# One PSUM pool, a fixed order in SyncE's queue, weights loaded early and masks by product in an RWKV-7 recurrence followed by a GELU layer

## The chip, the cores and the metric

One core of a Trainium2 chip runs the whole program. The metric is the time of one execution in microseconds (us), the median of the runs; beside it stands the span of a profiled execution, from its first instruction to its last.

## What is computed

The first half is a recurrence over 768 steps for 4 batches x 8 heads with a 40 x 40 state each, the second half a two-layer network on 3072 rows.

```python
for t in range(S):                                   # attention, per batch and head
    y[:, :, t] = np.einsum('bhd,bhde->bhe', rt, state)
    Sa = np.einsum('bhde,bhe->bhd', state, at)
    state_decay = state * wt[:, :, None, :] - np.einsum('bhd,bhe->bhde', Sa, bt)
    state = state_decay + np.einsum('bhd,bhe->bhde', vt, kt)
x = attn_out.transpose(0, 2, 1, 3).reshape(B * S, H * D)      # 3072 x 320
h = x @ w_in                                                  # 320 x 2048
out = (0.5 * h * (1.0 + erf(h / sqrt(2)))) @ w_out            # 2048 x 320
```

The two weight matrices arrive as 64-bit floats; the kernel loads their words and builds 32-bit floats on VectorE (`to_float`, seven instructions for each piece).

## The kernel before, in words

**Chunks.** The 768 steps are cut into 12 chunks of 64 (`NCH`). Inside a chunk the recurrence is written as products of small matrices: strictly upper triangular 64 x 64 blocks N, A, RV and M for each batch and head, made on TensorE in PSUM and masked on their way to SBUF (`masked`, line 313; the mask is `upper`), and the inverse of a unit triangular matrix made from N. Batches lie in pairs on the partitions (index e), heads in pairs (index x), so that one group of 32 products (64 hardware matmuls in the profile) handles all 32 batches and heads.

**Names.** `sums(c)` (L254) makes the running sum `cum` of log w and two exponentials of it. `turns(c)` (L286) transposes six tensors on TensorE (wT, aT, vT, nT, kT, rT), each copied from PSUM by ScalarE or VectorE, and starts the loads of v and r. `make_N`, `make_RV`, `make_A`, `make_av` are products that need the chunk's own data alone; `make_X`, `make_sa`, `make_M`, `make_y2`, `make_QY` and `outputs` need the state that the chunk before left. `turn_state` transposes the new state (tn). `up` is the first layer with GELU (ph, gt), `down(c, g)` the second for half of the rows (po, os).

**The inverse.** `make_N` sends N to DRAM (L345, 8 transfers) so that `invert` can read it back with one 32 x 32 block per partition (Nb, L377). GpSimd then does 62 instructions (L383, L385) on W, which goes to DRAM (inv, L389) and comes back as Tt and T2 (`fetch_inverse`, 12 transfers, L401 and L404). `corner` transposes a part of Tt on VectorE (L, L415) and multiplies (J); `joined` does the last products (J2) and completes Tt.

**What sets the order.** TensorE's instructions stand in the order of the program. All other engines, SyncE's queue of transfers among them, are ordered by the scheduler, which moves an instruction up when it can; each queue then runs in that order, and an instruction that waits holds all behind it. The loop over chunks (L591) is a software pipeline: in iteration c the state part of chunk c, the inverse of chunk n = c + 1, and the loads, sums and transposes of chunk c + 2.

**Memory.** PSUM holds three double banks for everything (`ps_duo`) and one for the two layers (`ps_fc`); `up` uses the halves of the latter's banks in turn (L552). `pad_ring` gives three padded tiles in turn to a, v, r and cs.

**Weights.** `first_weights` (L227) loads the five parts of w_in through a scratch of two and converts each; `second_weights` (L241) does the same for 16 parts of w_out through two buffers.

Of the kernel before, what the change touches and what calls it, by code (L numbers as in the profile page):

```python
# [11 lines left out]
INT32 = mybir.dt.int32  # L12
# [10 lines left out]
def kernel(  # L23
# [46 lines left out]
    P = 128  # L70
# [16 lines left out]
    ps_duo = ctx.enter_context(tc.tile_pool(name="ps_duo", bufs=3, space=PSUM))  # L87
    ps_fc = ctx.enter_context(tc.tile_pool(name="ps_fc", bufs=1, space=PSUM))

    def duo(name):  # L90
        return ps_duo.tile([P, 2, 512], FP32, tag="duo", name=name)
# [31 lines left out]
    pad_ring = ring("pad", 3, [P, G, H, HP], pads, nc.gpsimd)  # L123
# [14 lines left out]
    def fetch_padded(c, n, src, eng, placed):  # L138

        t = pad_ring()  # L140
# [10 lines left out]
    def load(c, other):  # L151
        fetch(c, "w", w, nc.sync)
        fetch_padded(c, "a", a, other, False)
        fetch(c, "k", k, nc.sync)
        fetch(c, "b", b, nc.sync)

    load(0, nc.scalar)
# [15 lines left out]
    mask = upper.bitcast(INT32)  # L173
# [5 lines left out]
    N_ring = ring("N", 1, [P, 2, G, NP, C], whole, nc.gpsimd)  # L179
    A_ring = ring("A", 1, [P, 2, G, NP, C], whole, nc.gpsimd)  # L180
    VR_ring = ring("VR", 2, [P, 2, G, NP, VC], lambda t: t.rearrange("p y g m c -> p (y g m) c")[:, :, D:], nc.gpsimd)
    SM_ring = ring("SM", 1, [P, 2, G, NP, VC], lambda t: t.rearrange("p y g m c -> p (y g m) c")[:, :, D:], nc.gpsimd)
# [26 lines left out]

    def to_float(dst, words):  # L210
# [16 lines left out]
    def first_weights():  # L227
        wide = moe_w_in.dtype != FP32
        src = (moe_w_in.bitcast(UINT32) if wide else moe_w_in).rearrange("k (p x j) -> k x p j", x=2, p=NF // 2)
        scratch = gt_tile().rearrange("p f t -> p (f t)").bitcast(UINT32)  # L230
        for kt in range(NK):
            dst = w_in_sb[:, kt]
            n = 2 * LW if wide else LW
            to = scratch[:, kt % 2 * n:(kt % 2 + 1) * n] if wide else dst
            for x, at, rows, feature in halves_of(kt):
                nc.sync.dma_start(out=to[x * HP + at:x * HP + at + rows].rearrange("p (f j) -> p f j", f=NF // 2),
                                  in_=src[feature:feature + rows, x])
            if wide:
                to_float(dst, to)

    def second_weights():  # L241
        wide = moe_w_out.dtype != FP32
        src = moe_w_out.bitcast(UINT32) if wide else moe_w_out
        for f in range(NF):
# [9 lines left out]
    def sums(c):  # L254
# [3 lines left out]
        for g in range(G):  # L258
            mm(cum[:, g], cum_m, logw[:, g].rearrange("p h d -> p (h d)"))
        rw = part_ring()[:, :, :DM]  # L260
        nc.scalar.activation(rw, cum, ACT.Exp, scale=-1.0)  # L261
        cs = pad_ring()
        nc.vector.tensor_copy(cs[:, :, :, :D], cum.rearrange("p g (h d) -> p g h d", h=H))  # L263
# [22 lines left out]
    def turns(c):  # L286
# [9 lines left out]
        fetch_padded(c, "v", v, nc.sync, True)  # L296
        v_ = raws.pop((c, "v"))
        VR = VR_ring()
        for g in range(G):
            nc.gpsimd.tensor_copy(VR[:, :, g, :, :D], v_[:, g, :, :D].rearrange("p (m y) d -> p y m d", y=2))  # L300
        vT = side("vT", "late", 1)
        nc.vector.tensor_copy(vT, flip(by_place(v_), "vT_ps"))
        nT = side("nT", "nT", 1)
        nc.scalar.copy(nT, flip(by_pair(nb), "nT_ps"))
        kT = side("kT", "kT", 1)
        nc.scalar.copy(kT, flip(by_pair(ks), "kT_ps"))
        fetch_padded(c, "r", r, nc.sync, True)
        rT = side("rT", "rT", 2)
        nc.vector.tensor_copy(rT, flip(by_place(raws.pop((c, "r"))), "rT_ps"))  # L309
        turned_in[c] = dict(ks=ks, nb=nb, wp=wp, aT=aT, vT=vT, nT=nT, kT=kT, rT=rT, VR=VR)  # L310


    def masked(to, pt):
        nc.vector.copy_predicated(to, mask.unsqueeze(1).to_broadcast([P, 2 * G * NP, C]), pt)
# [38 lines left out]
    def make_A(c):  # L353
        t = turned_in[c]
        A = t["A"] = A_ring()
# [13 lines left out]
    def invert(c):  # L369
# [9 lines left out]
        for j in range(BL - 1):  # L379
# [5 lines left out]
            nc.gpsimd.tensor_tensor(W[:, :rows, j + 1:], W[:, :rows, j + 1:], t, ALU.add)  # L385
        inv = dram.tile([2, 2, 2, G * NP, BL, BL], FP32, tag="inv", name="inv")
# [269 lines left out]
```

## Time and profile before

| what | value |
|---|---|
| median of 3 runs | 1113.56 us (1107.23 to 1120.38) |
| the profiled execution's own time | 1114.27 us |
| its span | 1112.3 us |
| TensorE busy | 796.9 us |
| VectorE, ScalarE, GpSimd busy | 311.6, 222.2, 339.4 us |
| mean granted TensorE clock | 0.86 |

A row of a timeline reads: start, duration, engine, line, operation, output<-inputs, partitions and shape, count, and in brackets the idle time before it with what ended it. Rows of the same kind that follow each other are merged. `SPq` is SyncE's queue: the time in which it issues transfers, not in which they run. A hardware matmul count is twice the program's, since a product of 32-bit floats runs as two. A row of waits reads: who waited, for whom, us in total, times, longest.

### The profile page before, as it was taken

The page shows a single profiled execution, that of the slowest core. Times are in us where ns is not written, and L with a number is a line of the kernel's source. Part 1 is how long each engine was busy: PE and PEld are TensorE (multiplying, and loading weights), DVE is VectorE, ACT ScalarE, POOL GpSimd, SP SyncE. Part 2 cuts the span into 40 slices and gives each one's busy share as a digit, 9 for nine tenths or more (in the row PEclk, how much of TensorE's full clock was granted, in tenths as well). Part 3 has the DMA queues.
Part 4 walks back from the last instruction along what each step waited for, and adds up shares of the span by engine and source line. Part 5 has one row for each costly group of instructions (what it writes and reads, how often), then busy time and mean ns, then how long its engine had stood idle before and what let it go on. Part 6 is the DMA issues. An engine that isn't in the chain of part 4 may idle for free.

```text
span 1112.3 us, 29772 instructions
## 1 busy us (share of the span) xinstructions
PE 796.9 (72%) x13256; PEld 637.2 (57%) x13256; DVE 311.6 (28%) x414; ACT 222.2 (20%) x282; POOL 339.4 (31%) x846
## 2 busy tenths in 40 slices
PE   4100565678878878788797787796886897787887
PEld 4100553476666665576585575675675685575765
DVE  2607495540140240240240240240330240240200
ACT  2000211211311311311311311311311311211110
POOL 5560036008007017016026026035035026025000
PEclk9555679779989989889889889889889889889899
DMA  5419452430330431331331331421321321111000
GB/s 90 86 35 130 96 132 69 97 71 13 68 69 13 72 72 21 61 73 19 63 68 22 65 63 24 70 56 27 68 54 25 68 57 22 25 44 21 16 19 13
DMA packets 255248, 60.41 MB, mean 54 GB/s; under 512 B 241232, under 2 KB 250960, under 8 KB 255120
## 3 DMA queue, kind: packets, MB, share of 16 engines
q1 hardware_dynamic: 251040, 56.22, 27.2%
q10 hardware_dynamic: 4080, 2.30, 1.0%
q8 instruction: 104, 1.70, 0.6%
q14 instruction: 24, 0.20, 0.1%
HBM read 44.30 MB, written 10.22 MB: 49 GB/s over the span
## 4 chain that ended last, share of the span: by engine, by line
PE 38%; POOL 20%; DMA 12%; SPq 11%; issue 9%; DVE 5%; ACT 4%; DVEq 0%; POOLq 0%; ACTq 0%
PE po L568 14%; POOL W L385 10%; POOL tmp L383 10%; PE ph L559 7%; SPq L146 3%; DMA Nb<-N 3%; SPq L345 2%; PE cum L100 2%; DMA pad<-in_r_dram 2%; SPq L401 2%; PE J L100 2%; DMA inv<-W 2%; PE N_ps L100 2%; ACT gt L556 2%; DMA Tt<-inv 2%
## 5 line engine op out<-in xcount | busy, mean ns | idle before, releaser
L559 PE MATMUL ph<-xt,w_in_sb 64*128 64x256 f32 x1920 | 235.5, 389 | 70.2 <-ACT gt L556 58.8
L559 PEld LDWEIGHTS ph<-xt,w_in_sb 64*128 64x128 f32 x1920 | 179.5, 188 | 127.1 <-ACT gt L556 92.6
L568 PE MATMUL po<-w_out_sb,gt 128*128 128x320 f32 x768 | 225.6, 454 | 1.3 <-ACT gt L556 0.7
L568 PEld LDWEIGHTS po<-w_out_sb,gt 128*128 128x128 f32 x768 | 154.0, 202 | 69.4 <-issue 13.2
L383 POOL TENSOR_TENSOR tmp<-W,Nb 128x126 f32<-128x126 f32 (+22 forms) x372 | 142.9, 384 | 153.0 <-DMA Nb<-N 125.5
L385 POOL TENSOR_TENSOR W<-W,tmp 128x126 f32<-128x126 f32 (+22 forms) x372 | 147.7, 397 | 29.1
L556 ACT ACTIVATE gt<-ph 128x512 f32<-128x512 f32 x96 | 57.4, 598 | 290.2 <-PE ph L559 275.1
L300 POOL COPY VR<-pad 128x320 f32<-128x320 f32 x24 | 11.3, 469 | 316.2 <-PE QY L100 294.2
L100 PE MATMUL cum<-w_raw,cum_m 128*128 128x320 f32 x48 | 29.0, 757 | 84.7 <-DMA k_raw<-in_k_dram 84.7
L415 DVE STREAM_TRANSPOSE L<-Tt 128x512 f32<-128x512 f32 x12 | 8.5, 711 | 278.5 <-DMA Tt<-inv 278.5
L100 PEld LDWEIGHTS cum<-w_raw,cum_m 128*128 128x128 f32 x48 | 13.5, 309 | 89.8 <-ACT w_raw L256 75.5
L570 DVE COPY os<-po 128x320 f32<-128x320 f32 x24 | 11.8, 492 | 182.7 <-PE po L568 182.7
L291 POOL TENSOR_TENSOR ks<-k_raw,part 128x640 f32<-128x640 f32 x12 | 18.5, 1542 | 140.0 <-ACT part L261 140.0
L100 PE MATMUL J<-L,N 32*32 32x32 f32 x768 | 11.7, 223 | 65.3 <-DVE L L415 65.3
L100 PEld LDWEIGHTS J<-L,N 32*32 32x32 f32 x768 | 10.5, 136 | 69.8 <-issue 69.8
L271 PE MATMUL rT_ps<-ident,pad 128*128 128x128 f32 x96 | 18.6, 327 | 32.1 <-DMA pad<-in_r_dram 31.6
L256 ACT ACT_TABLE_LOAD x12 | 15.4, 1283 | 107.4 <-DMA w_raw<-in_w_dram 107.4
L100 PE MATMUL QY<-VR,ks 64*64 64x104 f32 x768 | 27.9, 285 | 8.9 <-issue 7.2
L271 PEld LDWEIGHTS rT_ps<-ident,pad 128*128 128x128 f32 x96 | 12.3, 164 | 36.9 <-issue 26.0
L100 PEld LDWEIGHTS QY<-VR,ks 64*64 64x64 f32 x768 | 24.3, 156 | 10.3 <-issue 8.2
L309 DVE COPY rT<-rT_ps 128x1024 f32<-128x1024 f32 x12 | 14.7, 1225 | 52.9 <-PE rT_ps L271 52.9
L263 DVE COPY pad<-cum 128x640 f32<-128x640 f32 x12 | 9.9, 825 | 68.6 <-ACT part L261 68.6
(107 smaller groups left out, 1025.9 us busy)
## 6 DMA issues: line engine op xcount, KB each, us to landing
Nb<-N SPq DMA_DIRECT2D x24, 256.0 KB
wo_raw<-in_moe_w_out_dram SPq DMA_DIRECT2D x16, 320.0 KB
w_raw<-in_w_dram SPq DMA_DIRECT2D x48, 80.0 KB
k_raw<-in_k_dram SPq DMA_DIRECT2D x48, 80.0 KB
b_raw<-in_b_dram SPq DMA_DIRECT2D x48, 80.0 KB
pad<-in_v_dram SPq DMA_DIRECT2D x96, 40.0 KB
pad<-in_r_dram SPq DMA_DIRECT2D x96, 40.0 KB
out_dram<-os SPq DMA_DIRECT2D x48, 80.0 KB
```

Of the source, the lines that this page charges most:

```text
L100: nc.tensor.matmul(o, lhsT, rhs, start=first, stop=True, skip_group_check=True)
L146: eng.dma_start(out=t[half(e), g, y::2, :D], in_=rows[:, NP * y:NP * (y + 1)])
L256: nc.scalar.activation(logw, logw, ACT.Ln)
L271: nc.tensor.transpose(pt[:, g, n], src(g, n), ident)
L291: nc.gpsimd.tensor_tensor(ks[:, :, :, :D], raws.pop((c, "k")), rwv, ALU.mult)
L345: nc.sync.dma_start(out=blk[x, e, z].rearrange("n s t -> s n t"), in_=N[at:at + BL, x, :, :, z * BL:(z + 1) * BL].rearrange("p g n t -> p ...
L383: nc.gpsimd.tensor_tensor(t, W[:, :rows, j:j + 1].to_broadcast([P, rows, rest]), Nb[:, j:j + 1, j + 1:].to_broadcast([P, rows, rest]), ALU ...
L385: nc.gpsimd.tensor_tensor(W[:, :rows, j + 1:], W[:, :rows, j + 1:], t, ALU.add)
L401: nc.sync.dma_start(out=flat_T[at + z * BL:at + (z + 1) * BL, x, :, z * BL:(z + 1) * BL], in_=inv[x, e, z].rearrange("n s t -> s n t"))
L556: nc.scalar.activation(gt[:, 2 * p:2 * p + 2], ph, ACT.Gelu)
L559: nc.tensor.matmul(o, lhsT, rhs, start=kt == 0, stop=kt == NK - 1)
L568: nc.tensor.matmul(po, gts[c][:, f, g * P:(g + 1) * P], w_out_sb[:, f], start=f == 0, stop=f == NF - 1)
```

## The change

- **PSUM:** one pool of four double banks for everything. `up` takes a double bank for two groups of columns (a group is 10 matmuls of the program), with one GELU of 1024 columns where two of 512 were; each `down` takes one too.
- **SyncE's order:** its queue is taken out of the scheduler's hands and runs in the program's order. `load` is cut into w and a, k and b, v, r; `turns` into `turns_a` (what N needs) and `turns_b`; W goes to DRAM in `fetch_inverse`.
- **Pads:** a, cs, v and r have a padded tile each.
- **Weights:** the first two parts of w_in and v are loaded ahead of chunk 0's `sums`, the other parts between the loads of chunk 1, all ahead of the first inverse's result; w_out is loaded in pieces of 4, 4 and 8 inside iteration 0.
- **Masks:** `masked` multiplies by `upper` in place of a predicated copy into a zeroed tile; the memsets of N, VR and SM go, and A shares its memory with nT.
- **The loop:** N before X, `sums` and the second `down` before `corner`, `turn_state` after the transposes, and `fetch_inverse` after `sums`.

```diff
-    ps_duo = ctx.enter_context(tc.tile_pool(name="ps_duo", bufs=3, space=PSUM))
-    ps_fc = ctx.enter_context(tc.tile_pool(name="ps_fc", bufs=1, space=PSUM))
+    psum = ctx.enter_context(tc.tile_pool(name="psum", bufs=4, space=PSUM))
...
-    pad_ring = ring("pad", 3, [P, G, H, HP], pads, nc.gpsimd)
+    padded = {n: ring(n + "_pad", 1, [P, G, H, HP], pads, nc.gpsimd) for n in ("a", "cs", "v", "r")}
...
-    load(0, nc.scalar)
+    ctx.enter_context(tc.manual_schedule(engines={mybir.EngineType.PE, mybir.EngineType.SP}))
+    load_wa(0, nc.scalar)
+    load_kb(0)
...
     def masked(to, pt):
-        nc.vector.copy_predicated(to, mask.unsqueeze(1).to_broadcast([P, 2 * G * NP, C]), pt)
+        nc.vector.tensor_tensor(to, pt, upper.unsqueeze(1).to_broadcast([P, 2 * G * NP, C]), ALU.mult)
...
-        inverses[c] = inv
+        inverses[c] = W
 
     def fetch_inverse(c):
-        inv = inverses[c]
+        W = inverses[c]
+        n = P // 2
+        inv = dram.tile([2, 2, 2, G * NP, BL, BL], FP32, tag="inv", name="inv")
+        rows = inv.rearrange("x e z n (s q) t -> q (x e z n) s t", q=2)
+        for par in range(2):
+            nc.sync.dma_start(out=rows[par], in_=W[par * n:(par + 1) * n])
...
-        fc = ps_fc.tile([P, 2, 2, TB], FP32, tag="fc", name="ph")
-        for p in range(NF // 2):
-            ph = fc[:, :, p % 2]
-            for kt in range(NK):
-                for x in range(2):
-                    mm_up(ph[:, x], w_in_sb[half(x), kt, p * P:(p + 1) * P], xt[half(x), kt], kt)
-            nc.scalar.activation(gt[:, 2 * p:2 * p + 2], ph, ACT.Gelu)
+        for q in range(NF // 4):
+            ph = duo("ph").rearrange("p x (s t) -> p x s t", s=2)
+            for s in range(2):
+                p = 2 * q + s
+                for kt in range(NK):
+                    for x in range(2):
+                        mm_up(ph[:, x, s], w_in_sb[half(x), kt, p * P:(p + 1) * P], xt[half(x), kt], kt)
+            nc.scalar.activation(gt[:, 4 * q:4 * q + 4].rearrange("p (s x) t -> p x s t", x=2), ph, ACT.Gelu)
...
+    first_load(0)
+    first_load(1)
+    load_v(0)
     sums(0)
-    turns(0)
+    turns_a(0)
     make_N(0)
     invert(0)
-    first_weights()
+    load_r(0)
+    turns_b(0)
     make_RV(0)
     make_A(0)
     make_av(0)
-    load(1, nc.sync)
+    first_convert(0)
+    first_load(2)
+    first_convert(1)
+    load_wa(1, nc.sync)
+    load_kb(1)
+    first_load(3)
     sums(1)
-    turns(1)
+    turns_a(1)
+    load_v(1)
+    first_convert(2)
+    first_load(4)
+    load_r(1)
+    turns_b(1)
+    first_convert(3)
+    first_convert(4)
     fetch_inverse(0)
     corner(0)
     joined(0)
-    second_weights()
+    second_weights(0, 4)
     for c in range(NCH):
         n = c + 1
-        more = n < NCH
-        make_X(c)
+        more, more2 = n < NCH, n + 1 < NCH
         if more:
             make_N(n)
             invert(n)
+        if more2:
+            load_wa(n + 1, nc.sync)
+        make_X(c)
+        if more:
             make_RV(n)
         make_sa(c)
         if more:
-            fetch_inverse(n)
             make_A(n)
         make_M(c)
         make_y2(c)
         make_QY(c, 0)
         make_QY(c, 1)
+        if c == 0:
+            second_weights(4, 8)
         outputs(c)
         if more:
             make_av(n)
+        if c == 0:
+            second_weights(8, NF)
         if c:
             down(c - 1, 1)
+        if more2:
+            load_kb(n + 1)
+            load_v(n + 1)
+            load_r(n + 1)
         up(c)
+        if more2:
+            sums(n + 1)
+        if more:
+            fetch_inverse(n)
+        down(c, 0)
         if more:
             corner(n)
-        if n + 1 < NCH:
-            load(n + 1, nc.sync)
-            sums(n + 1)
-        down(c, 0)
+        if more2:
+            turns_a(n + 1)
+            turns_b(n + 1)
         if more:
             turn_state()
-        if n + 1 < NCH:
-            turns(n + 1)
-        if more:
             joined(n)
```

What this moves is read best from the order of the instructions on three stretches. Line numbers with the change are those of the changed file.

TensorE in the middle of a period, before, from the second layer of the chunk before to the last transpose (po and ph: second and first layer; J: `corner`):

```order
L568 MATMUL po<-w_out_sb,gt 128x320 x16
L559 MATMUL ph<-xt,w_in_sb 128x256 x80
L100 MATMUL J<-L,N_118 32x32 x32
L100 MATMUL cum<-w_raw,cum_m 128x320 x2
L568 MATMUL po<-w_out_sb,gt 128x320 x16
L271 MATMUL tn_ps<-ident,st_132 128x128 x8
L271 MATMUL wT_ps<-ident,pad_71 128x128 x8
```

and now:

```order
L578 MATMUL po<-w_out_sb,gt 128x320 x16
L573 MATMUL ph<-xt,w_in_sb 128x256 x80
L98 MATMUL cum<-w_raw,cum_m 128x320 x2
L578 MATMUL po<-w_out_sb,gt 128x320 x16
L98 MATMUL J<-L,N_119 32x32 x32
L282 MATMUL wT_ps<-ident,cs_pad_68 128x128 x8
```

J, the first product that needs the inverse, has moved behind cum and the second po; tn has moved to the end of the transposes.

SyncE's queue over a period, before, from the loads of a chunk to the write of the inverse:

```order
L135 DMA w_raw<-in_w_dram 64x8x40 x4
L135 DMA k_raw<-in_k_dram 64x8x40 x4
L135 DMA b_raw<-in_b_dram 64x8x40 x2
L573 DMA out_dram<-os 64x320 x2
L148 DMA pad_71<-in_a_dram 64x8x40
L146 DMA pad_69<-in_r_dram 64x4x40 x8
L148 DMA pad_71<-in_a_dram 64x8x40 x3
L135 DMA b_raw<-in_b_dram 64x8x40 x2
L146 DMA pad_69<-in_v_dram 64x4x40 x8
L345 DMA N<-N_118 32x8x32 x8
L377 DMA Nb<-N 64x1024 x2
```

and now, from N to the write of the inverse:

```order
L357 DMA N<-N_119 32x8x32 x8
L389 DMA Nb<-N 64x1024 x2
L133 DMA w_raw<-in_w_dram 64x8x40 x4
L146 DMA a_pad_66<-in_a_dram 64x8x40 x4
L533 DMA xt<-xt 24x1024
L536 DMA xt<-xt 16x256 x4
L583 DMA out_dram<-os 64x320 x2
L133 DMA k_raw<-in_k_dram 64x8x40 x4
L133 DMA b_raw<-in_b_dram 64x8x40 x4
L144 DMA v_pad_70<-in_v_dram 64x4x40 x8
L144 DMA r_pad_72<-in_r_dram 64x4x40 x8
L406 DMA inv<-W 1024x1x32 x2
```

All loads of a chunk have moved from ahead of N to behind Nb, and k, b, v and r stand directly ahead of the inverse's write.

SyncE's queue at the start, before, from the last parts of w_in to the first read of the inverse (its write stands ahead of all of these):

```order
L236 DMA gt<-in_moe_w_in_dram 16x8x256 x8
L135 DMA w_raw<-in_w_dram 64x8x40 x4
L148 DMA pad_71<-in_a_dram 64x8x40 x4
L135 DMA k_raw<-in_k_dram 64x8x40 x4
L135 DMA b_raw<-in_b_dram 64x8x40 x4
L146 DMA pad_69<-in_v_dram 64x4x40 x8
L146 DMA pad_71<-in_r_dram 64x4x40 x8
L401 DMA Tt_128<-inv 32x8x32 x2
```

and now:

```order
L144 DMA v_pad_70<-in_v_dram 64x4x40 x8
L245 DMA gt<-in_moe_w_in_dram 16x8x256 x8
L144 DMA r_pad_72<-in_r_dram 64x4x40 x8
L406 DMA inv<-W 1024x1x32 x2
L414 DMA Tt_123<-inv 32x8x32 x2
```

The loads have moved ahead of the inverse's write, which its read now follows directly.

84 lines of the change are left out of this document (42 added, 42 removed).

## The prediction

> **What bounds the kernel now.** I read the engines' busy times on the page first, then the windows of the span cut at two places (length, then busy time of each engine, granted clock, DMA share, GB/s), then TensorE's timeline in one period, then the inverse through the other engines' timelines, and last the start.
>
> ```profile
> PE 796.9 (72%) x13256; PEld 637.2 (57%) x13256; DVE 311.6 (28%) x414; ACT 222.2 (20%) x282; POOL 339.4 (31%) x846
> ...
> 0.00:233.30 233.30, 91.70 (x1508) 75.79 (x1512) 116.99 (x179) 35.72 (x42) 77.70 (x172) 0.68 0.48 91
> 233.30:976.20 742.90, 592.98 (x10056) 474.72 (x10052) 173.92 (x207) 168.89 (x213) 238.26 (x612) 0.90 0.26 49
> 976.20:1112.30 136.10, 112.19 (x1716) 86.69 (x1708) 20.73 (x28) 17.57 (x27) 23.44 (x62) 0.95 0.11 23
> ```
>
> No engine is full, TensorE at 72% included: what bounds is a loop of waits. The cuts are the starts of N_ps of chunk 2 and of chunk 11, so the middle is nine periods of 742.9/9 = 82.5 us; 233.3 us lie ahead and 136.1 behind. One period on TensorE:
>
> ```profile
> 533.26 1.08 PE L100 MATMUL J<-L,N 32*32 32x32 f32 x64 [4.64 <-DVE L L415]
> 534.27 2.50 PE L100 MATMUL cum<-w_raw,cum_m 128*128 128x320 f32 x4
> 536.56 9.84 PE L568 MATMUL po<-w_out_sb,gt 128*128 128x320 f32 x32
> 546.24 1.04 PE L271 MATMUL tn_ps<-ident,st 128*128 128x128 f32 x8
> 547.12 1.04 PE L271 MATMUL wT_ps<-ident,pad 128*128 128x128 f32 x8
> ...
> 558.04 1.95 PE L100 MATMUL X<-st,aT 40*64 40x40 f32 x64
> 559.77 1.97 PE L100 MATMUL N_ps<-aT,nT 40*64 40x64 f32 x64
> ...
> 576.46 8.88 PE L568 MATMUL po<-w_out_sb,gt 128*128 128x320 f32 x32
> ...
> 589.08 2.43 PE L559 MATMUL ph<-xt,w_in_sb 64*128 64x256 f32 x20 [0.72 <-ACT gt L556]
> 592.20 1.13 PE L559 MATMUL ph<-xt,w_in_sb 64*128 64x256 f32 x8 [0.70 <-ACT gt L556]
> ...
> 615.63 1.08 PE L100 MATMUL J<-L,N 32*32 32x32 f32 x64 [5.37 <-DVE L L415]
> ```
>
> (The row at 592.20 is cut by its window.) From N_ps at 559.77 to J at 615.63 are 55.9 us, and there TensorE waits for L, thus for the inverse; from J to the next N_ps are 26.5. Their sum is the period. The 55.9 belong to the inverse:
>
> ```profile
> 561.80 1.29 DVE L314 COPY_PREDICATED N<-upper,N_ps 128x1024 f32<-128x1024 int32 x1 [0.86 <-PE N_ps L100]
> ...
> 558.02 6.85 SPq L146 DMA_DIRECT2D pad<-in_v_dram  x8
> 564.97 4.73 SPq L345 DMA_DIRECT2D N<-N  x8
> ...
> 605.12 1.29 SPq L389 DMA_DIRECT2D inv<-W  x2
> 606.52 1.26 SPq L573 DMA_DIRECT2D out_dram<-os  x2
> ...
> 577.07 0.56 POOL L383 TENSOR_TENSOR tmp<-W,Nb 128x31 f32<-128x31 f32 x1 [3.83 <-DMA Nb<-N]
> ```
>
> The mask ends at 563.1, the transfer of N starts at 564.97 behind v's loads, GpSimd works from 577.1 to 605.1 (28), and 10.5 us of transfers and a transpose lead to J.
>
> **The change, part by part.** *The period.* The change does not shorten the inverse; it moves work under it. cum and the second po now stand ahead of J, X behind N_ps, r and v have pads of their own, and tn comes last. Between J and the next N_ps stay J 1.0 (533.26 to 534.27), seven transposes at 0.88 (546.24 to 547.12) = 6.2 and the joining products, 0.9 (up to 558.04): 8.1. I add 0.9 for the waits between transposes, of which the one that stays took up to 0.8 (nT for ScalarE, quoted below): **9 us for 26.5**.
>
> Ahead of J, TensorE now does: the small products of N_ps to av, one po, ph, cum, the other po. The small products:
>
> ```profile
> 639.37 1.01 PE L100 MATMUL X<-st,aT 40*64 40x40 f32 x53
> 641.48 0.54 PE L100 MATMUL X<-st,aT 40*64 40x40 f32 x10 [1.10 <-issue]
> ...
> 661.23 2.96 PE L568 MATMUL po<-w_out_sb,gt 128*128 128x320 f32 x10
> ...
> PE ph L559 <- ACT gt L556: 58.8, 84, 0.7
> ...
> PE nT_ps L271 <- ACT wpT L293: 7.4, 9, 0.8
> ```
>
> 18.4 us in the period above (558.04 to 576.46), 21.9 here (639.37 to 661.23), where TensorE stands for "issue" in between; I take 20. po is 8.9. In ph twelve more matmuls take 2.43 - 1.13 = 1.30 us, 108 ns each, so its 160 take 17.3 without pauses. The pauses are 0.70 us eight times: TensorE waits for Gelu though the two groups use different halves of the banks. With four double banks a group of two fills one and Gelu empties another. Gelu of 1024 columns isn't in the trace; one of 512 is:
>
> ```profile
> 591.55 0.60 ACT L556 ACTIVATE gt<-ph 128x512 f32<-128x512 f32 x1 [2.53 <-PE ph L559]
> ...
> 550.70 1.23 DVE L295 TENSOR_TENSOR aT<-aT_ps,wpT 128x1024 f32<-128x1024 f32 x1 [3.76 <-ACT wpT L293]
> ```
>
> So between 0.6 and 1.2; I take 1.1, hidden under 4.3 us of matmuls, as either end is. cum at full clock is about 1.2 (2.29 here behind an idle stretch; the po behind it, 9.7, shows the same). Sum: 20 + 8.9 + 17.3 + 1.2 + 8.9 = **56.3**.
>
> The inverse's side: v no longer stands ahead of N (1.9 us less), so GpSimd ends 43.5 us behind N_ps instead of 45.3. But SyncE now keeps the program's order, and k, b, v and r stand between an output transfer and inv. That output waits for po: 20 + 8.9 + about 0.5 for the copy to SBUF + 1.3 issue (606.52) = 30.7.
>
> ```profile
> 540.57 2.63 SPq L135 DMA_DIRECT2D k_raw<-in_k_dram  x4
> 548.97 5.30 SPq L146 DMA_DIRECT2D pad<-in_r_dram  x8
> ```
>
> k 2.6, b 2.6, v 5.3 to 6.9, r 5.3: SyncE comes to inv at 46.5 to 48, 3 to 4.5 us after GpSimd. Behind it the 10.5 us stay: J at 57 to 58.5. I take 57.5, one us later than TensorE: no long idle. Behind L on VectorE stand cs, nb and os in a fixed queue, and J and the first transposes run meanwhile; if they don't cover them, it is part of the 0.9 above. **Period 57.5 + 9 = 66.5 us.** If cover went, the first to be late would be TensorE at J: each us there is nine.
>
> *Masks by product* are not in the trace: the predicated copy of this size takes 1.29, a product of a PSUM tile with an SBUF tile (aT, above) 1.23. I take 1.23, the same form, and the other row as the other end; only N's mask lies on the chain, so 0.1 us a period or none. The fewer table loads (three for four a period) and memsets are hidden.
>
> *The start.*
>
> ```profile
> 131.13 1.07 PE L100 MATMUL J<-L,N 32*32 32x32 f32 x64 [4.68 <-DVE L L415]
> ...
> 133.70 1.99 PE L100 MATMUL N_ps<-aT,nT 40*64 40x64 f32 x64
> ...
> 76.01 1.31 SPq L389 DMA_DIRECT2D inv<-W  x2
> 77.42 20.81 SPq L236 DMA_DIRECT2D gt<-in_moe_w_in_dram  x16
> 123.79 1.10 SPq L401 DMA_DIRECT2D Tt<-inv  x2
> ...
> 190.44 0.33 DVE L218 TENSOR_SCALAR low<-wo_raw 128x320 uint32<-128x320 uint32 x1 [12.06 <-DMA wo_raw<-in_moe_w_out_dram]
> ...
> 193.93 0.33 DVE L218 TENSOR_SCALAR low<-wo_raw 128x320 uint32<-128x320 uint32 x1
> ```
>
> The first inverse is written at 76.0 and read back from 123.8, since 16 weight loads and all of chunk 1 stand between. Now these stand ahead: behind Nb (at about 34, as before: two parts of w_in ahead of N, r no longer) r, the three other parts of w_in and w, a, k, b, v, r of chunk 1 are 56 issues of 0.6 to 0.9, about 40 us, so inv goes at about 74, Tt 3.4 later, and 6 us for it. VectorE must end a conversion ahead of L, some 3 us: J of chunk 0 at 87 instead of 131.1, N_ps of chunk 1 at 89 instead of 133.7. **44 us won.** The stretch up to N_ps of chunk 2 took 99.6 and stays near that: the second weights in turns of two buffers hold SyncE (16 conversions of 3.5 us, 190.44 to 193.93, with chunk 0's masks and outputs between them 4.4: from 88 to 158; the last load goes two before, at about 152), behind them 24 loads of 16 us, then inv at 168, J 10.5 later at 179, N_ps 10 later at **189** for 233.3.
>
> *The end.* Chunk 11 has no loads behind it: N_ps to J 55.5 (20 + 8.9 + 17.3 + 8.9). Behind J:
>
> ```profile
> 1042.45 1.14 PE L100 MATMUL X<-st,aT 40*64 40x40 f32 x64
> 1055.43 8.88 PE L568 MATMUL po<-w_out_sb,gt 128*128 128x320 f32 x32
> 1099.40 8.88 PE L568 MATMUL po<-w_out_sb,gt 128*128 128x320 f32 x32 [0.58 <-DVE os L570]
> ```
>
> J, tn and joining 3.5, the small products 13.0 (1042.45 to 1055.43), three po 26.6, ph 17.3, the last output 4.0 (1108.3 to 1112.3): 64.5. Together 120 for 136.1.
>
> **Sum: 189 + 9 x 66.5 + 120 = 907.5 us of span.** The execution's own time is 1114.27 for a span of 1112.3, and the median 1113.56, so 2 us more: **909 us**.
>
> **A rule against it.** Where the trace shows TensorE standing for "issue" among the small products, those gaps return in other places whatever the clock; I take them as the stage's own pace. The Trainium skill's page "Runtime: NRT & Kernel Launch", section on instruction fetch mechanics, says that refilling an engine's instructions is mostly hidden. By that rule the small products would follow their matmuls; the 1.10 us above speaks against it, and no run here shows the fetch itself. What it would make of the time is (a).
>
> **The rivals.**
> (a) The gaps vanish: eleven products at 1.1 us (X here: 1.01 for 53 of 64) plus waits for masks are 13, loads end by 41, GpSimd by 43, J comes at 53.5, with TensorE idle for 4 us before it. Period 63, time 876.
> (b) SyncE is later than I count. With J at 61 TensorE stands 4 us and restarts at a half clock, as cum does above; two transposes then cost 1.8 more. Period 72, time 958. For it: v's loads took 6.85 once.
> (c) The start gives nothing: with the order fixed, SyncE stands in second_weights while N's transfer waits behind. N_ps of chunk 2 stays near 230: 950.
> (d) The pool doesn't free TensorE: ph keeps its pauses, 7.7 us more on a path that is as long as the chain. Period 73, time 974.
> (e) Slower: the fixed queue becomes the clock. Each of the 24 loads then waits for an earlier one to land, and inv goes only behind them. It decides from a period of 89 on, that is J at 80 and 40 us for the 24 loads, 1.65 each against 0.66 to 0.86: then 1112. At 1.8 each it is 1144. Nothing in the rows shows such loads in mid-run.
>
> **How the numbers follow.** Forecast 0.54, (a) 0.12, (b) 0.15, (c) 0.10, (d) 0.05, (e) 0.04. The forecast alone spans 885 to 935 (period 64 to 69). The range 870 to 960 takes in (a), (b) and (c) and leaves out (d) and (e). A measurement of this kernel can tell about 1% from no change; only (e) is not faster by that: faster 0.95, within 1% 0.02, slower 0.03.
>
> **What would show it.** N_ps starts 65 to 68 us apart; ph in one run of 160 matmuls of 17 to 18 us without Gelu's pauses; J after po with a wait under 3 us; inv issued by SyncE right behind r's loads and later than GpSimd's end; N_ps of chunk 2 at 180 to 200. J waiting over 4 us, with a half clock behind, would be (b); N_ps of chunk 2 beyond 220, (c). A period over 75 would prove the reckoning wrong.

## The result and the profile after

| | before | after |
|---|---|---|
| median | 1116.19 us of 4 runs (1107.23 to 1120.38) | **937.50 us** of 4 runs (935.61 to 946.43) |
| ratio | | 0.842, 95% interval 0.835 to 0.850 |
| profiled execution, its span | 1114.27, 1112.3 us | 936.90, 935.2 us |
| mean granted TensorE clock | 0.86 | 0.86 |

Every ratio here and below is taken from the executions within 1.5% of each kernel's fastest, beside executions of the kernel before from the same session.

The forecast was 909 us (870 to 960). The kernel is faster by the mechanism that was forecast, and 28 us slower than the sum said. The page's line of TensorE, and the windows cut at the same two places as before, the starts of N_ps of chunk 2 and of chunk 11 (columns: length, busy time of PE, PEld, DVE, ACT, POOL, granted clock, DMA share, GB/s):

```profile
PE 759.0 (81%) x13256; PEld 640.0 (68%) x13256; DVE 301.5 (32%) x414; ACT 199.2 (21%) x225; POOL 341.8 (37%) x842
...
0.00:191.50 191.50, 90.13 (x1448) 76.01 (x1448) 114.97 (x178) 30.85 (x34) 74.62 (x168) 0.68 0.55 104
191.50:814.70 623.20, 561.45 (x10046) 476.74 (x10044) 165.67 (x207) 151.18 (x172) 243.82 (x612) 0.90 0.33 60
814.70:935.20 120.50, 107.41 (x1780) 87.30 (x1768) 20.89 (x30) 17.14 (x21) 23.34 (x62) 0.95 0.12 26
```

So 177.1 us of span went: 41.8 at the start (233.3 to 191.5), 119.7 in the nine periods (82.5 to 623.2/9 = 69.25 us each) and 15.6 at the end (136.1 to 120.5). Start and end came out 2.5 and 0.5 us above the forecast; the period was forecast at 66.5, and nine times 2.75 us is the rest of the miss. One period on TensorE:

```profile
467.50 1.16 PE L98 MATMUL N_ps<-aT,nT 40*64 40x64 f32 x64
...
475.56 1.65 PE L98 MATMUL saT_ps<-Tt,part 64*64 64x64 f32 x50 [1.31 <-issue]
...
488.77 8.88 PE L578 MATMUL po<-w_out_sb,gt 128*128 128x320 f32 x32
497.58 17.54 PE L573 MATMUL ph<-xt,w_in_sb 64*128 64x256 f32 x160
515.05 1.34 PE L98 MATMUL cum<-w_raw,cum_m 128*128 128x320 f32 x4
516.23 8.78 PE L578 MATMUL po<-w_out_sb,gt 128*128 128x320 f32 x32
527.63 1.08 PE L98 MATMUL J<-L,N 32*32 32x32 f32 x64 [2.63 <-DVE L L428]
528.64 1.97 PE L282 MATMUL wT_ps<-ident,cs_pad 128*128 128x128 f32 x8
...
534.78 1.04 PE L282 MATMUL vT_ps<-ident,v_pad 128*128 128x128 f32 x8
...
538.17 1.16 PE L98 MATMUL N_ps<-aT,nT 40*64 40x64 f32 x64
```

cum and the second po stand ahead of J now, ph is one run of 160 matmuls without a pause, and J still waits for L, 2.63 us here. Behind that wait the first transposes take 1.97 us, the later ones 1.04: the granted clock was 0.50 from 527.6 to 533.8 and 0.98 behind it. The same period in SyncE's queue, and GpSimd's last instruction of the inverse:

```profile
498.21 1.17 SPq L583 DMA_DIRECT2D out_dram<-os  x2
499.47 3.81 SPq L133 DMA_DIRECT2D k_raw<-in_k_dram  x4
503.33 2.67 SPq L133 DMA_DIRECT2D b_raw<-in_b_dram  x4
506.10 5.24 SPq L144 DMA_DIRECT2D v_pad<-in_v_dram  x8
511.44 5.70 SPq L144 DMA_DIRECT2D r_pad<-in_r_dram  x8
517.24 1.27 SPq L406 DMA_DIRECT2D inv<-W  x2
```

```profile
509.64 0.23 POOL L397 TENSOR_TENSOR W<-W,tmp 128x16 f32<-128x16 f32 x1
```

The inverse is ready at 509.9 and leaves at 517.2, right behind r's loads: SyncE is 7.4 us late here. Over nine periods the lateness is 2.7 to 7.4, 4.8 in the mean; in chunk 11, which has no loads behind it, inv leaves as GpSimd ends. ScalarE's row shows that the pool does its part (a Gelu of 1024 columns, waiting for ph and not the other way):

```profile
502.22 1.02 ACT L570 ACTIVATE gt<-ph 128x1024 f32<-128x1024 f32 x1 [6.62 <-PE ph L573]
```

The start: inv of chunk 0 is written at 79.1 and read back at once, where the kernel before wrote it at 76.0 and read it back at 123.8.

```profile
79.10 1.27 SPq L406 DMA_DIRECT2D inv<-W  x2
83.06 0.82 SPq L414 DMA_DIRECT2D Tt<-inv  x2
...
90.26 1.08 PE L98 MATMUL J<-L,N 32*32 32x32 f32 x64 [8.05 <-DVE L L428]
```

### The profile page after: what moved, and what is told of

Same layout as the page of the kernel before. It is cut to its first block, busy times and chain, and to the rows that moved or that the text cites. A ratio compares the mean times of both kernels' runs of the same rounds, so it can differ in the third digit from the quotient of the medians.

```text
span 935.2 us, 29736 instructions
## 1 busy us (share of the span) xinstructions
PE 759.0 (81%) x13256; PEld 640.0 (68%) x13256; DVE 301.5 (32%) x414; ACT 199.2 (21%) x225; POOL 341.8 (37%) x842
## 4 chain that ended last, share of the span: by engine, by line
PE 52%; SPq 14%; DMA 11%; issue 8%; POOL 6%; DVE 6%; ACT 2%; DVEq 0%; POOLq 0%; ACTq 0%
PE ph L573 15%; PE po L578 13%; SPq L144 5%; PE QY L98 4%; POOL W L397 3%; POOL tmp L395 3%; DMA inv<-W 3%; SPq L414 3%; DMA Tt<-inv 2%; DMA gt<-in_moe_w_in_dram 2%; SPq L133 2%; PE aT_ps L282 2%; SPq L357 2%; PE y_ps L98 2%; PE M_ps L98 2%
## 5 line engine op out<-in xcount | busy, mean ns | idle before, releaser
L573 PE MATMUL ph<-xt,w_in_sb 64*128 64x256 f32 x1920 | 212.1, 379 | 19.0 <-DMA xt<-xt 19.0
L573 PEld LDWEIGHTS ph<-xt,w_in_sb 64*128 64x128 f32 x1920 | 187.0, 188 | 44.3 <-DVE low L231 19.1
L578 PE MATMUL po<-w_out_sb,gt 128*128 128x320 f32 x768 | 212.8, 435 | 2.1 <-DVE w_out_sb L233 2.1
L578 PEld LDWEIGHTS po<-w_out_sb,gt 128*128 128x128 f32 x768 | 144.9, 190 | 62.7 <-DVE w_out_sb L233 2.6
L570 ACT ACTIVATE gt<-ph 128x1024 f32<-128x1024 f32 x48 | 49.2, 1024 | 222.4 <-PE ph L573 222.4
L302 POOL TENSOR_TENSOR ks<-k_raw,part 128x640 f32<-128x640 f32 x12 | 24.3, 2024 | 86.6 <-ACT part L274 86.6
L98 PEld LDWEIGHTS J<-L,N 32*32 32x32 f32 x768 | 9.2, 120 | 54.3 <-issue 53.1
L526 DVE TENSOR_TENSOR y<-QY,y 128x512 f32<-128x512 f32 x22 | 15.1, 686 | 54.1 <-PE QY L98 42.0
L98 PE MATMUL cum<-w_raw,cum_m 128*128 128x320 f32 x48 | 18.4, 512 | 12.2 <-DMA k_raw<-in_k_dram 9.3
L318 POOL COPY VR<-v_pad 128x320 f32<-128x320 f32 x24 | 11.1, 472 | 44.4 <-DMA v_pad<-in_v_dram 44.4
L98 PE MATMUL M_ps<-rT,saT 40*64 40x64 f32 x768 | 22.3, 261 | 5.9 <-issue 4.3
L98 PE MATMUL saT_ps<-Tt,part 64*64 64x64 f32 x704 | 20.2, 271 | 6.9 <-issue 6.9
```

What stands on the lines that cost most here:

```text
L98: nc.tensor.matmul(o, lhsT, rhs, start=first, stop=True, skip_group_check=True)
L302: nc.gpsimd.tensor_tensor(ks[:, :, :, :D], raws.pop((c, "k")), rwv, ALU.mult)
L570: nc.scalar.activation(gt[:, 4 * q:4 * q + 4].rearrange("p (s x) t -> p x s t", x=2), ph, ACT.Gelu)
L573: nc.tensor.matmul(o, lhsT, rhs, start=kt == 0, stop=kt == NK - 1)
L578: nc.tensor.matmul(po, gts[c][:, f, g * P:(g + 1) * P], w_out_sb[:, f], start=f == 0, stop=f == NF - 1)
```

## The experiments

Two theories stood against each other. **A:** the period is the inverse's chain, and SyncE, which issues k's, b's, v's and r's loads ahead of inv, lengthens it by the lateness seen above, and by the half clock behind J's wait. **B:** TensorE's own path up to J is nearly as long, so that a shorter queue brings nothing. Then the parts of the change were undone or done alone. The table gathers what the runs' profiles show; the means are over the nine periods from the starts of N_ps, J and inv and the end of GpSimd's last instruction.

| run | median us | ratio to before (95%) | N_ps of chunk 2 | period | N_ps to J | J to N_ps | N_ps to GpSimd's end | inv behind that end |
|---|---|---|---|---|---|---|---|---|
| before | 1116.2 | | 233.3 | 82.5 | 56.5 | 26.0 | 46.0 | 0.0 |
| after | 937.5 | 0.842 (0.835 to 0.850) | 191.5 | 69.2 | 59.2 | 10.0 | 43.8 | 4.8 |
| kb_early | 901.4 | 0.806 (0.802 to 0.809) | 191.3 | 65.7 | 58.1 | 7.6 | 43.5 | 0.7 |
| two_pools | 981.0 | 0.876 (0.872 to 0.881) | 193.9 | 72.4 | 64.7 | 7.7 | 43.1 | 5.7 |
| sp_scheduled | 990.8 | 0.885 (0.880 to 0.889) | 175.3 | 77.2 | 64.9 | 12.4 | 53.1 | 0.0 |
| predicated | 935.5 | 0.834 (0.830 to 0.839) | 192.6 | 68.6 | 59.1 | 9.5 | 43.6 | 4.9 |
| before_pool4 | 1112.4 | 0.995 (0.992 to 0.998) | 234.4 | 83.0 | 56.6 | 26.5 | 46.0 | 0.0 |
| kbv_mid | 907.5 | 0.811 (0.807 to 0.816) | 193.7 | 65.8 | 57.7 | 8.1 | 43.7 | 1.9 |
| moved | 916.9 | 0.818 (0.812 to 0.825) | 193.8 | 66.4 | 58.2 | 8.2 | 42.0 | 4.9 |
| spread | 891.5 | 0.796 (0.792 to 0.801) | 192.2 | 63.7 | 55.4 | 8.4 | 43.2 | 1.3 |
| inv_first | 962.1 | 0.863 (0.859 to 0.867) | 216.9 | 69.8 | 59.7 | 10.1 | 43.8 | 5.2 |
| spread_start | 889.3 | 0.796 (0.792 to 0.800) | 175.9 | 64.6 | 56.6 | 8.0 | 43.5 | 2.0 |
| moved_start | 908.4 | 0.814 (0.810 to 0.818) | 172.6 | 67.5 | 59.4 | 8.2 | 42.7 | 5.5 |
| spread_n2 | 888.7 | none | 174.3 | 64.6 | 56.5 | 8.1 | 42.2 | 3.1 |

### kb_early: k and b ahead of the wait

```diff
             load_wa(n + 1, nc.sync)
+            load_kb(n + 1)
...
-            load_kb(n + 1)
             load_v(n + 1)
             load_r(n + 1)
```

> The changed kernel with k's and b's eight loads for the chunk after next moved in SyncE's queue from behind the output transfer to right behind a's loads, so that only v and r stand between the output and inv. Theory A (the inverse's chain through SyncE's queue sets the period): SyncE then comes to inv at about GpSimd's end and not 4.8 us behind it; J's wait of 2.6 us a period goes, and with it the half clock of the first transposes, period 69.25 -> about 66, time 937 -> 900 to 912. Rival B (TensorE's own path and the VectorE work ahead of L set the period, the wait only shows which came last): inv comes earlier but the period stays within 0.7 us, 930 to 940. Rival C: xt's transfer, now behind k and b, comes later and ph with it: 940 to 950.

Measured 901.39 us: theory A. J follows po without a wait, and the transposes behind it run at full clock:

```profile
503.04 8.78 PE L578 MATMUL po<-w_out_sb,gt 128*128 128x320 f32 x32
511.75 0.75 PE L98 MATMUL J<-L,N 32*32 32x32 f32 x64
512.43 1.09 PE L282 MATMUL wT_ps<-ident,cs_pad 128*128 128x128 f32 x8
```

J does not wait for L in any of the nine periods. Of the 3.5 us that a period lost, 2.4 lie between J and the next N_ps (10.0 to 7.6): most of it is the half clock, 0.4 of it waits of the second transpose for ScalarE. Only 1.1 lie between N_ps and J, since TensorE's own path is the next to come. In this order that path is what bounds, as theory B has it.

### two_pools: the pools of before in the changed kernel

```diff
-    psum = ctx.enter_context(tc.tile_pool(name="psum", bufs=4, space=PSUM))
+    ps_duo = ctx.enter_context(tc.tile_pool(name="ps_duo", bufs=3, space=PSUM))
+    ps_fc = ctx.enter_context(tc.tile_pool(name="ps_fc", bufs=1, space=PSUM))
...
-        for q in range(NF // 4):
+        fc = ps_fc.tile([P, 2, 2, TB], FP32, tag="fc", name="ph")
+        for p in range(NF // 2):
```

> The changed kernel with the PSUM pools, up and down of before: three double banks for the small products, one for ph and po, a Gelu for every two groups of 256 columns. Theory A (TensorE's own path is within 2.6 us of the chain, and ph's pauses of 0.7 us eight times plus a wait of the small products for a third buffer lie on it): 4 to 7 us a period and 3 at the end, 937 -> 975 to 1010. Rival B (the inverse's chain is the clock, TensorE has room for the pauses because SyncE's queue holds inv anyway): under 2 us a period, 937 to 957.

Measured 981.03: theory A. ph's pauses are back, and J comes behind po without a wait: TensorE is the clock, at 72.4. 28.6 of the 45 us of span are in the nine periods, 14.2 at the end. The time lies in A's range, but its parts do not: a period is 3.2 us longer, not 4 to 7, since the half clock behind J goes too (10.0 to 7.7), and the end is 14.2 longer, not 3, since two runs of ph stand in it, each 24.3 us long for 17.5.

```profile
519.82 2.43 PE L573 MATMUL ph<-xt,w_in_sb 64*128 64x256 f32 x20 [0.70 <-ACT gt L570]
...
547.70 0.75 PE L99 MATMUL J<-L,N 32*32 32x32 f32 x64
```

### sp_scheduled: SyncE's order left to the scheduler

```diff
-    ctx.enter_context(tc.manual_schedule(engines={mybir.EngineType.PE, mybir.EngineType.SP}))
+    ctx.enter_context(tc.manual_schedule(engines={mybir.EngineType.PE}))
```

> The changed kernel with SyncE's order left to the scheduler; it puts the loads of the chunk after next (w, k, b, a, v, r, 28 issues) ahead of N's transfer and nothing between xt and inv. Theory A (the order decides, and inv's place is what costs 4.8 us): inv leaves at GpSimd's end, but N's transfer stands behind r's loads, which can't start before r's buffer is free, so Nb comes later by 3 to 8 us and the period is 67 to 73: 915 to 975. Rival B (the fixed order is what made the gain; without it TensorE waits as before): above 1000.

Measured 990.83, above A's bound and just below B's. A's mechanism is there, under-sized: inv leaves as GpSimd ends (table: 0.0), but N's transfer, whose mask ends at 486.25 in this period, starts at 494.18: the loads of w, k, b, a and v and the first of r stand ahead of it. GpSimd ends 53.1 us behind N_ps for 43.8, nine later and not 3 to 8.

```profile
485.02 1.23 DVE L326 TENSOR_TENSOR N<-N_ps,upper 128x1024 f32<-128x1024 f32 x1
...
486.32 6.09 SPq L144 DMA_DIRECT2D v_pad<-in_v_dram  x8
492.51 1.57 SPq L144 DMA_DIRECT2D r_pad<-in_r_dram  x1
494.18 5.10 SPq L357 DMA_DIRECT2D N<-N  x8
```

What the fixed order is worth, 53 us, is net: the scheduler's start is 16 us earlier.

### predicated: three masks as before

```diff
-        masked(flat(N), products("N_ps", t["nT"], t["aT"], True))
+        predicated(flat(N), products("N_ps", t["nT"], t["aT"], True))
```

(and RV and M likewise, into tiles zeroed once)

> The changed kernel with three of the four masks (N, RV, M) as predicated copies into tiles zeroed once, as before; A's mask stays a product. Theory A (0.08 us for each, only N's lies on the chain, 0.1 us a period): 936 to 940, no change that can be measured. Rival B (the products are worth more than their own length, since the masks end the small products' waits): above 946.

Measured 935.46: no difference that can be measured, theory A. The copies take 1.30 us, the product 1.22.

### before_pool4: the pool alone

The kernel before with the pool, `up` and `down` of the change and nothing else.

> The kernel of before with one edit: one PSUM pool of four double banks and the up and down that go with it (ph in groups of four, Gelu of 1024 columns). Theory A (a faster ph pays only where TensorE's own path is as long as the inverse's chain; in the kernel before J waits 5 us for L already): ph loses its pauses of 0.7 us, J waits that much longer, 1100 to 1125, nothing or 1%. Rival B (the pool is worth the same wherever it stands, 44 us in the changed kernel by the run with two pools): 1065 to 1080.

Measured 1112.43, 0.5% faster (0.2 to 0.8%): theory A. What is worth 44 us in the changed kernel is worth 0.5% alone. ph is as fast as in the change, 17.5 us for 24.3, but J waits that much longer, so a period is no shorter (83.0 for 82.5); only the end, with its two runs of ph, is (129.6 us for 136.1):

```profile
594.21 17.54 PE L559 MATMUL ph<-xt,w_in_sb 64*128 64x256 f32 x160
622.11 1.08 PE L99 MATMUL J<-L,N 32*32 32x32 f32 x64 [10.37 <-DVE L L414]
```

### kbv_mid: k, b and v between xt and the output

```diff
         if more2:
+            load_kb(n + 1)
+            load_v(n + 1)
+        if c:
+            down(c - 1, 1)
+        if more2:
             load_r(n + 1)
```

> As the run with k and b early, but k's, b's and v's loads stand between xt's transfer and the output's, so that nothing new stands ahead of xt and r alone between the output and inv. In the run with k and b early (901) TensorE has no wait for L left and waits for xt ahead of ph, some 0.5 to 0.9 us a period. Theory A (that wait is k's and b's, and TensorE is now the clock): 892 to 898. Rival B (xt comes from VectorE's end, the queue ahead of it is empty by then): 899 to 904. Rival C (r alone behind a later output makes inv late again): above 906.

Measured 907.45, in C's range but not for C's reason. The intervals of this run's ratio and kb_early's meet. inv is 1.9 us late again, as C said, but that costs nothing at J, which waits for L in none of the nine periods. The waits of ph for xt are gone, as A said (27.4 us over kb_early; the 18.8 here lie all in chunk 0), but A's gain is not there: the period stays at 65.8. N_ps to J is only 0.4 us shorter, as the small products from N_ps to av take 21.3 us for 20.8, and J to N_ps is 0.5 longer, with waits of the second transpose for ScalarE in two periods (0.93 and 0.70 us). Why these moved was not tried.

### moved and spread: the gaps among the small products

With J's wait gone, TensorE's own gaps are on the path. Two of them in kb_early:

```profile
455.80 0.44 PE L98 MATMUL RV_ps<-rT,vT 40*64 40x64 f32 x14
457.37 0.97 PE L98 MATMUL RV_ps<-rT,vT 40*64 40x64 f32 x50 [1.13 <-issue]
458.12 1.13 PE L98 MATMUL sap<-part,Tt 64*64 64x40 f32 x64
459.03 0.48 PE L98 MATMUL saT_ps<-Tt,part 64*64 64x64 f32 x14
460.99 0.97 PE L98 MATMUL saT_ps<-Tt,part 64*64 64x64 f32 x48 [1.49 <-issue]
```

From one gap to the next are 50 + 64 + 14 = 128 matmuls; each has a weight load, so 256 instructions. Two kernels put the first po of a chunk off into the next period, one whole, one in pieces. Both also have k and b early, v ahead of the output and cum ahead of ph, so each differs from kb_early in several things, and from the other in the pieces alone:

```diff
         make_X(c)
+        if c:
+            down(c - 1, 0)
         if more:
             make_RV(n)
...
-        down(c, 0)
```

```diff
         make_X(c)
+        parts = down_parts(c - 1, 0) if c else iter(())
+        next(parts, None)
         if more:
             make_RV(n)
+        next(parts, None)
-        make_sa(c)
+        make_sa(c, parts)
+        for _ in parts:
+            pass
```

> From the run with k and b early (901, period 65.7): the first po of a chunk is put off into the next period, whole, right behind X; cum ahead of ph; v's loads between xt and the output. TensorE does the same work between N_ps and J. Theory A (128 matmuls of the trace among the small products end in a gap of 1.1 to 1.8 us put down to issue, since the instructions of a matmul of 0.02 us can't be brought as fast as they run): the whole po lets one block come in time, one gap of four goes, period 63.5 to 65, 880 to 897; also earlier at the start, since the weights of the first po may come later. Rival B (the gaps belong to the products' own pace): 65 to 66, 893 to 903.

> As the run with the po moved, but that po's 32 matmuls are cut into four pieces, behind X, RV, sap and saT. The same instructions in another order. Theory A (supply of instructions): each piece gives 2.2 us to bring the next block, the gaps among RV, sap and saT go (two of 1.1 to 1.8 us), 2 to 3 us a period less than with the po whole: 855 to 880, until J waits for L again (the inverse's chain alone is 53.6 from N_ps to J, period about 61.5). Rival B (own pace): as the run with the po moved, within 0.5 us a period.

Measured 916.88 and 891.54. The first is a miss for both theories: with the po put off whole it is slower than kb_early. The table's row fits this account, which was not tried alone: the later small products make xt, the output and so inv later (4.9 us), and J waits for L again, 19.6 us over the nine periods for none in kb_early. The second is above A's bound (J waits for L 18.5 us there), but 25 us below the first. Because SyncE's lateness differs between the two, the pair is repeated below with r's place changed. From N_ps to the end of av TensorE took 28.7 us with the po whole and 25.7 in pieces, in the mean.

### inv_first: the start undone

inv of chunk 0 is written right behind `load_r(0)`, ahead of the parts of w_in and chunk 1's loads; it is read back where it was.

```diff
     load_r(0)
+    write_inverse(0)
     turns_b(0)
```

> The changed kernel with one step of the start put back: inv of chunk 0 is written right behind r's loads, ahead of the three last parts of w_in and of chunk 1's loads, so that these wait in SyncE's queue until GpSimd has finished the first inverse; its reading back stays where it is. Theory A (the start's gain is these transfers standing ahead of the wait for GpSimd): J of chunk 0 at 120 to 132 for 90.3, N_ps of chunk 2 some 25 to 42 us later than 191.5, the period unchanged, 937 -> 962 to 980. Rival B (the conversions on VectorE and the second weights hold the start, and catch up the delay by N_ps of chunk 2): 937 to 950.

Measured 962.06: theory A, at the low end, and J's 120 to 132 was too late. SyncE waits for GpSimd until 64.5 and then issues for 40 us; J of chunk 0 comes at 114.3, N_ps of chunk 2 25.4 us late, and the median is 24.6 us later.

```profile
64.51 1.27 SPq L406 DMA_DIRECT2D inv<-W  x2
...
99.19 6.35 SPq L144 DMA_DIRECT2D r_pad<-in_r_dram  x8
105.58 1.09 SPq L420 DMA_DIRECT2D Tt<-inv  x2
```

### spread_start and moved_start: a shorter start, and the pair again

```diff
+        if c == 1:
+            second_weights(12, NF)
...
-        if c == 0:
-            second_weights(8, NF)
         if more2:
             load_v(n + 1)
+            load_r(n + 1)
+        if c == 1:
+            down(c - 1, 0)
         if c:
             down(c - 1, 1)
...
+        if c == 0:
+            second_weights(8, 12)
```

> From the run with the po spread (892; N_ps of chunk 2 at 192, periods of 63.7): the last eight loads of w_out go behind the read-back of chunk 1's inverse and behind chunk 2's N, the first po goes whole into chunk 1's end, and r stands ahead of the output's transfer. In the spread run TensorE waits 26 us for L at chunk 1's J and 15.5 for xt, with SyncE held by w_out's loads. Theory A (SyncE's queue, held by the two buffers of w_out, sets the start): N_ps of chunk 2 at 168 to 178, and inv no longer 1 to 2 us late, period 62.5 to 63.5: 860 to 880. Rival B (the conversions only move: VectorE is late for chunk 2's masks and po waits for w_out): N_ps of chunk 3 as late as before, 886 to 895.

Measured 889.31, not told from spread: rival B as to the start. N_ps of chunk 2 is 16 us earlier (175.9), that of chunk 3 only 1.7 (251.2 for 252.9): the first period takes 75.3 us for 60.7, with VectorE busy 34.7 us in it for 18.9 and TensorE waiting for w_out's last parts. From chunk 3 on the period is 63.2 for 64.1.

moved_start differs from it in one thing, the po whole behind X:

> The last run (po spread, start and r's place changed, 889) with one edit back: the put-off po stands whole behind X and not in four pieces. In the first pair, po whole against po in pieces, SyncE also came 4 to 6 us late to inv in the first and under 2 us in the second, so that the 25 us between them were not the gaps' alone; here r stands ahead of the output in both. From the start of N_ps to the end of av TensorE took 28.6 us with po whole and 24.5 in pieces. Theory A (the gaps, supply of instructions): those 4 us come back, TensorE reaches J at about 55 instead of 50.5 behind N_ps, L is there at 53 to 54, period 1 to 2 us longer: 898 to 912. Rival B (the 25 us were SyncE's lateness): 885 to 895.

Measured 908.41, 19 us more: theory A. The same instructions, first with the po whole, then in four pieces:

```profile
516.23 8.88 PE L579 MATMUL po<-w_out_sb,gt 128*128 128x320 f32 x32
525.04 1.16 PE L98 MATMUL RV_ps<-rT,vT 40*64 40x64 f32 x64
526.02 1.09 PE L98 MATMUL sap<-part,Tt 64*64 64x40 f32 x64
526.93 0.77 PE L98 MATMUL saT_ps<-Tt,part 64*64 64x64 f32 x34
529.66 0.63 PE L98 MATMUL saT_ps<-Tt,part 64*64 64x64 f32 x25 [1.96 <-issue]
```

```profile
512.88 2.42 PE L579 MATMUL po<-w_out_sb,gt 128*128 128x320 f32 x8
515.23 1.22 PE L98 MATMUL saT_ps<-Tt,part 64*64 64x64 f32 x64
516.38 2.42 PE L579 MATMUL po<-w_out_sb,gt 128*128 128x320 f32 x8
518.73 1.16 PE L98 MATMUL A_ps<-aT,kT 40*64 40x64 f32 x64
...
524.01 0.85 PE L98 MATMUL QY<-VR,ks 64*64 64x104 f32 x28 [1.39 <-issue]
```

With pieces between them the products from RV to y follow each other without a gap; QY and av keep theirs (1.39 and 1.47 us in this period). The granted clock is 1.00 from 506.0 to 530.0. With the po whole saT has its gap, and the clock is 0.80 from 516 to 541. N_ps to the end of av took 28.6 us against 25.6, in the mean of the eight periods in which this po stands there. xt, the output and inv follow these products, so SyncE's lateness differs again (5.5 against 2.0). As both kernels have the same queue, it is taken for a consequence of the gaps and not a cause beside them.

### spread_n2: N's transfers on two queues

```diff
-                    nc.sync.dma_start(out=blk[x, e, z].rearrange("n s t -> s n t"),
+                    (nc.scalar if z else nc.sync).dma_start(out=blk[x, e, z].rearrange("n s t -> s n t"),
```

> The last run (po spread, start and r's place changed, 889, periods of 63.2 from chunk 3 on) with four of N's eight transfers on ScalarE's queue instead of SyncE's. J waits for L again, 45 us over the run, so the inverse's chain is the clock there. Theory A (the eight issues of 4.6 us lie on the chain): Nb 2.3 us earlier, so inv and J too, as long as SyncE comes to inv in time; period 61 to 62, 866 to 876. Rival B (Nb waits for the transfers' landing, or SyncE's loads then are what comes last ahead of inv, by 1 to 2 us): under 0.7 us a period, 882 to 892.

Measured 888.71 us; the six executions lay apart (875 to 890), so no ratio is given, and the trace decides: rival B. GpSimd ends 1.3 us earlier behind N_ps than in spread_start, inv leaves only 0.2 earlier: SyncE comes to it 3.1 us late in the mean, behind v, r and the output, all of which stand behind xt. Here W's last instruction ends at 539.1:

```profile
523.94 0.83 SPq L534 DMA_DIRECT2D xt<-xt  x1
...
533.22 5.67 SPq L144 DMA_DIRECT2D r_pad<-in_r_dram  x8
538.98 1.20 SPq L586 DMA_DIRECT2D out_dram<-os  x2
540.27 1.26 SPq L406 DMA_DIRECT2D inv<-W  x2
```

The best versions are the three with the po spread, 889 to 892 us, a ratio of 0.796 to before for the two that have one; they are not told apart by these runs.

## Why the prediction was right, point by point

- **The loop of waits and what is moved under it: right.** N_ps to J grew by 2.7 us (56.5 to 59.2) and J to N_ps shrank by 16. Cuts, kind of wait and place came as written: J waits for L 1.5 to 2.9 us in eight of the nine periods (3.2 in the last), inv stands right behind r's loads, and N_ps of chunk 2 lies between 180 and 200. The period (69.25) missed its 65 to 68.
- **The mis-sized term: N_ps to J, "57.5, one us later than TensorE: no long idle", and behind it "J to N_ps 9".** Measured 59.2 and 10.0. GpSimd's end (43.5 said, 43.8 found) and the stretch from inv to J (10.5 said, 10.6 found) were right. SyncE's lateness was said to be 3 to 4.5 and was 4.8: the output's issue ended 31.3 behind N_ps in the mean, for 30.7, and from there to inv passed 17.3 us in the mean (17.9 in the period shown), where the single rows gave 15.8 to 17.4. From 57 to 58.5, the lower half was chosen. kb_early shows that this is the cause: with 8 of the 24 loads moved the lateness falls to 0.7 and the period to 65.7, 36 us of median.
- **The half clock was put in the wrong place.** Rival (b) had it behind a wait of 4 us, the forecast without it. In the period shown it came behind 2.63 us: three transposes at 1.7 us from start to start for 0.87. It stands behind J's wait in eight of the nine periods, for waits of 1.76 to 3.18 us, and not behind the one of 1.49. (b) is thus half right: its mechanism, at a smaller wait. The Trainium skill's page "TensorE: Matmul & The Clock Gate", section on the HAM clock gate, gives at least one idle window of about 3.4 us as what throttles the clock; here TensorE waited 2.63 us, followed by J's 64 small matmuls in 1.08, and the clock was 0.50, so the measurement decides against reading it as a wait of that length. Nor does the length alone decide: in spread_start J waited 3.43 us once, and the clock was 1.00 from 370.6, where that J starts, to 377.5; what decides was not tried.
- **TensorE's own path to J, 56.3:** 58.1 in kb_early, where it bounds: the small products took 20.8 for 20, and 0.5 us in the mean (1.7 at most) went to waits for xt. So the room beside SyncE's delay was about a microsecond, as priced.
- **The pool: right, and it depends on the rest.** ph is one run of 17.5. (d) is refuted for the change, and its price was near: it gave 7.7 us more of ph, a period of 73 and 974 us, and two_pools, which has those pauses, came at 6.8, 72.4 and 981. before_pool4 shows that the pool alone moves only J's wait and, at the end, 6.5 us.
- **Masks: right,** nothing.
- **The start: right, with two misses that offset each other.** The 56 issues ahead of inv took 45.7 us for 40, so inv went at 79.1 for 74, J of chunk 0 came at 90.3 for 87 and N_ps of chunk 1 at 95.0 for 89; the stretch from there to N_ps of chunk 2 then took 96.5 us for 100, and that N_ps came at 191.5 for 189. inv_first gives back 25 of the 42 us, so the order of the loads against the first wait for GpSimd is most of it. That the rest is the reading back, which in the kernel before came only behind all weights, is argued from its rows and was not tried alone. (c) is refuted.
- **The end: right,** 120.5 for 120, from N_ps to J 56.9 for 55.5 and behind J 63.6 for 64.5. The terms written for the two parts add to 55.1 and 64.4, so 0.5 us of the 120 is a slip of the sum.
- **(a), the gaps vanish: refuted for this order,** and yet some of them can be made to vanish. The Trainium skill's page "Runtime: NRT & Kernel Launch", section on instruction fetch mechanics, says that instructions come in blocks of 16 KiB, 256 instructions, and that crossing a block is mostly hidden. The count of 256 agrees with the rows above, but hidden it is not: the gaps put down to issue add up to 45 us in the changed kernel. Here the traces show more than the prediction said ("no run here shows the fetch itself"). They list transfers of the kind "instruction", the one of the kernel before too; the first row is of the changed kernel's whole span, the second of the 0.1 us from 472.5 (queue, transfers, MB, share of 16 engines' time):

```profile
q8 instruction: 104, 1.70, 0.8%
...
q8 instruction: 1, 0.02, 95.4%
```

104 transfers of 16 KiB for 26,512 matmuls and weight loads are one for each 255 of them, so q8 is taken for TensorE's. The transfer that starts behind 472.5 takes 1.53 us by its share, ends at 474.1, and saT goes on at 475.56 after its gap of 1.31. This holds throughout: in the 14 traces together, 279 of TensorE's 280 gaps for issue longer than 1 us end 1.2 to 1.7 us after the end of such a transfer. So the gaps are waits for TensorE's own instructions. With longer matmuls between the products a block lands in time: in spread_start RV, sap and saT have no gap, QY and av keep theirs. Whether the data transfers of the same moments slow the fetch stays open.

- **(e), the fixed queue slower: refuted.** Left to the scheduler the same kernel is 53 us slower.

## What to carry to other kernels

Read a queue as part of the chain: loads that may go early belong behind the last wait that they can pass, not ahead of the transfer that the chain needs, and eight issues of 0.65 to 0.95 us moved here were worth 36 us. Price a wait with what the clock does behind it, over several periods. Where the smallest matmuls wait for their own instructions, put longer ones between them. And judge a part where the others stand: the pool alone was worth 0.5%, in the new order 44 us.

## What was not expected of the hardware

- TensorE's granted clock was 0.61 from 471.4 to 488.8 in the changed kernel, though TensorE was busy for 15.56 of these 17.40 us; a gap of 1.56 us ends where the stretch begins, and gaps of 1.31 and 0.51 lie in it. In spread_start the same products, with longer matmuls between some of them and a gap of 1.39, ran at 1.00. Whether the shorter idle time or the longer matmuls keep the clock up was not tried.
- Among products whose matmuls start every 0.02 us, a gap returns every 128 matmuls. From N_ps to the end of av TensorE took 20.8 us in kb_early. With 32 longer matmuls among them, whose 8.8 us are taken off, it took 19.8 where these stood in one piece (moved_start) and 16.8 where they stood in four (spread_start).
